# Token mix of a layer: half tiles of two batches on 64 rows each, in place of 128 rows with zeroed weights

## The chip, the cores and the metric

One core of one Trainium2 chip runs the whole program. The metric is device microseconds of one execution; the median of three runs of the kernel before is 675.2 us (674.82 to 675.28).

## What is computed

A masked attention, a gated feed-forward layer and a token-mixing layer follow one another. The part around the change is the first half of the last one, for 4 batches of 576 tokens and 512 channels:

```python
    xt = x.transpose(0, 2, 1)
    h = np.maximum(xt @ w_tok1, 0.0) @ w_tok2     # w_tok1 576 x 256, w_tok2 256 x 576
    u = x + h.transpose(0, 2, 1)
    h2 = np.maximum(u @ w_ch1, 0.0) @ w_ch2
    return (u + h2).astype(np.float32)
```

## The kernel before

**Tiles.** A float32 product is made of three matmuls on a high and a low part of each factor (mm3, line 453: high by high, high by low, low by high). The parts come from split (line 469): a copy to the high part on ScalarE (ACT) or VectorE (DVE), then a subtraction on DVE for the low part. The tokens of all batches lie in 18 tiles of 128 rows in x2. A batch has 576 tokens, four whole tiles and a half one; tile 8 holds the last 64 tokens of batch 0 in its rows 0 to 63 and those of batch 1 in its rows 64 to 127, tile 17 the same of batches 2 and 3.

**First product.** tokens_in(b) (line 892) sums w_tok1 by the tokens of a batch into two banks (hp, 128 x 512 each, m = 0 and 1) over five tiles: 6 matmuls a tile, 30 a batch. For the fifth tile there are two copies of the last 64 rows of w_tok1, each with 128 rows: t1[4] has the weights in rows 0 to 63 and zeroes below, t1[5] the other way round (lines 847 to 850; single, line 500, loads the rows and lets GpSimd (POOL) set the others to zero). So the whole half tile is multiplied, 128 rows, and what belongs to the other batch falls away. The relu of a bank is one instruction on ACT for the high part and one on DVE for the low part. In the trace the fifth tile's matmuls read wr (the split tile) with at (t1[4], batches 0 and 2) or with z (t1[5], batches 1 and 3).

**Around it.** turn(t) (line 914) transposes a token tile with four 128 x 128 transposes (cst,x or cst,y in the trace) and copies them to u. tokens_out(b) (line 929) is the second product, eight products of six matmuls with 288 columns (at,z in the trace), each added to u by DVE. The program writes them as: turns 0 to 3, tokens_in(0), turn 8, turns 4 to 7, tokens_in(1), tokens_out(0), turns 9 to 12, tokens_in(2), turn 17, tokens_out(1), turns 13 to 16, tokens_in(3), tokens_out(2), tokens_out(3).

**Order.** That is not the order of issue. All instructions go to a planner (class Plan). It knows what each depends on, and a planned cost for each (_cost, line 248). In order (line 294) every instruction of TensorE (PE) is first given the sum of the planned PE costs ahead of it in the program as its due time; then, from the back, every instruction is due no later than each of its readers less its own cost, a delay between the two engines and a pad. An engine that is free takes, of the instructions that are ready, the one with the earliest due time:

```python
            if e == "tensor":
                due[i], t = t, t + cost[i]
        for i in reversed(range(n)):
            pad = 0 if first[i] == "tensor" else 1.0
            for s in after[i]:
                due[i] = min(due[i], due[s] - cost[i] - self.TAIL[first[i]] - self.DELAY[first[i]][first[s]] - pad)
```

Only matmuls that are given to burst (line 237) stay together whatever their due times; the attention does so with its matmuls of 96 rows by 64 columns (weigh, line 620), which write the two column halves in turn. The chip's engines run their queues in the order that the planner has written.

Of the kernel before, what the change touches and what calls it, by code (L numbers as in the profile page):

```python
# [10 lines left out]
F32R = mybir.dt.float32r  # L11
# [3 lines left out]
AF = mybir.ActivationFunctionType  # L15
ALU = mybir.AluOpType
PSUM = bass.MemoryType.PSUM

B, H, S, D = 4, 8, 576, 64
C = H * D  # L20
NT = B * S
FF, HID, FF2 = 1024, 256, 1536
# [127 lines left out]
class Plan:  # L150
# [96 lines left out]
    @staticmethod  # L247
    def _cost(engine, method, kw):

        out = kw["out"]  # L250
        cols = int(np.prod(out.shape[1:]))
        pointers = sum(hasattr(kw.get(k), "space") for k in ("scale", "bias", "scalar", "scalar1"))
        if engine == "sync":
            if kw["in_"].dtype == U32:
                return max(0.45, 4 * cols * out.shape[0] / 230e3 - 0.9)
            return max(0.45, 8 * (0.03 + 4 * cols * 0.0266e-3))
        if engine == "tensor":
            if method == "transpose":
                return cols / 1200 + 0.0025
            if kw["lhsT"].dtype in (F32R, BF16):  # L260
                return cols / 2263 + 0.0049
            if kw["lhsT"].shape[0] <= D or out.shape[0] <= D:
                return cols / 1200 + 0.0025
            return 2 * max(cols / 1200 + 0.0025, 0.112)
        source = kw.get("in_", kw.get("in0"))
        psum = source is not None and "PSUM" in str(source.space)
        if engine == "scalar":
            read = 0.093 * (kw.get("accum_out") is not None)
            return (0.07 if psum else 0.1) + cols / 1200 + 0.03 * pointers + read
        if engine == "gpsimd":  # L270
            return 0.04 if method == "memset" else 0.04 + cols / 345
        if method == "tensor_reduce":
            return 0.066 + int(np.prod(source.shape[1:])) / 960
        if method == "reciprocal":
            return 0.066 + cols / 157
        fast = method in ("tensor_copy", "tensor_scalar", "tensor_scalar_add") and not psum
        return 0.066 + 0.05 * pointers + cols / (1920 if fast else 960)
# [147 lines left out]
def tile_model(nc, banks, kept_1, kept_w, kept_u, kept_mid, units, cst, mu, w_k, w_v, w_r, w_t1, w_t2, w_c1, w_c2, outT):  # L425
    memory = {k: [Slot(f"{k}{i}", n) for i, n in enumerate(v)] for k, v in SLOTS.items()}

    def f(view):
        return view.bitcast(F32)

    def at(place, shape, dtype=F32):
        name, number, offset = place
        return memory[name][number].view(offset, shape, dtype)
# [6 lines left out]
    def cut(name, numbers, size, count=None):  # L440

        out = []
        for n in numbers:
            out += [(name, n, size * i) for i in range(SLOTS[name][n] // size)]
        return out[:count]
# [7 lines left out]
    def mm3(out, lh, ll, rh, rl, first, last, goes_on=False):  # L453

        more = dict(skip_group_check=True) if goes_on else {}
        nc.tensor.matmul(out=out, lhsT=lh, rhs=rh, start=first, stop=False, **more)
        nc.tensor.matmul(out=out, lhsT=lh, rhs=rl, start=False, stop=False, **more)
        nc.tensor.matmul(out=out, lhsT=ll, rhs=rh, start=False, stop=last, **more)
# [10 lines left out]
    def split(raw, hi, lo):  # L469
        copy(hi, raw)  # L470
        combine(lo, raw, f(hi), ALU.subtract)

    def rows(n):
        return slice(128 * n, 128 * n + 128)
# [6 lines left out]
    def pair(place, shape):  # L481

        name, number, offset = place
        n = int(np.prod(shape))
        return at(place, shape, F32R), at((name, number, offset + n), shape, F32R)
# [3 lines left out]
    wr = [pair(("wr", k, 0), (C,)) for k in range(4)]  # L489
# [7 lines left out]

        return words(w).rearrange("(k p) c -> p k c", p=128)[:, :, 2 * n * m:2 * n * m + 2 * n]

    def single(srcs, t, raw_ring, zero=None):  # L500

        n = t.shape[1]
        flat = raw_ring.tile(2 * n, dtype=U32)
        for part, src in srcs:
            dst = flat[part]
            if len(src.shape) == 3:
                dst = dst.split(src.shape[1], src.shape[2])
            nc.sync.dma_start(out=dst, in_=src)
            if raw_ring is raw_a:
                nc.early[len(nc.ops) - 1] = 6  # L510
        if zero is not None:
            nc.gpsimd.memset(out=f(flat[zero]), constant=0.0)
        raw = flat.split(n, 2)
        low, h = raw[:, :, 0], raw[:, :, 1]
        b, half = t.bitcast(U32), t.bitcast(U16)
        v = nc.vector
        nc.scalar.activation(out=t, in_=f(h), func=AF.Prelu, scale=2.0 ** -112, alpha=-(2.0 ** 32))
        v.tensor_scalar(out=b, in0=b, scalar1=3, scalar2=None, op0=ALU.logical_shift_left)
        v.scalar_tensor_tensor(
            out=half, in0=low, scalar=2.0 ** -29, in1=half, op0=ALU.mult, op1=ALU.add  # L520
        )

    def weight(srcs, hi, lo, raw_ring, tmp_ring, zero=None):

        shape = tuple(hi.shape[1:])
        t = tmp_ring.tile(int(np.prod(shape)))
        single(srcs, t, raw_ring, zero)
        split(t.split(*shape) if len(shape) == 2 else t, hi, lo)

    everything = slice(0, 128)  # L530
# [121 lines left out]
    z512 = cut("z", range(5), 512)  # L652
# [4 lines left out]
    x2 = [at(place, (C,)) for place in x2_at]  # L657
# [180 lines left out]

    t1 = [pair(p, (HID,)) for p in cut("at", (1, 2), 512) + [("at", 0, 4 * S), ("at", 0, 4 * S + 512), z512[8]]]
    t2 = [pair(p, (S,)) for p in cut("at", (0,), 2 * S, 2)]
    xt512 = cut("xt", (2, 0, 1), 512)
    raw_b, tmp_b = ring(xt512[8:10]), ring(xt512[10:12])
# [1 line left out]
        weight([(everything, words(w_t1)[rows(k), :])], *t1[k], raw_b, tmp_b)  # L846
    tail = words(w_t1)[512:576, :]
    halves = [slice(0, 64), slice(64, 128)]
    for odd in range(2):
        weight([(halves[odd], tail)], *t1[4 + odd], raw_b, tmp_b, zero=halves[1 - odd])  # L850
    for k in range(2):
        for n in range(3):
            cs = slice(192 * n, 192 * n + 192)
# [8 lines left out]

    def u(b, kt, cs):
        return whole[kt // 2][:, kt % 2, S * b:S * b + S][:, cs]

    def tiles_of(b):
        base, odd = 9 * (b // 2), b % 2
        return [(base + 4 * odd + i, i) for i in range(4)] + [(base + 8, 4 + odd)]

    spots = cut("wk", range(4), 512) + cut("xt", (2, 0), 512) + cut("wr", (2,), 512) + cut("x2", (5, 6, 0, 1, 2, 3), 512)  # L870
    w1 = []
# [13 lines left out]

    for j in range(3):
        fetch_1(j)
    hid, ends = {}, {}
    hp_r, x2p_r, up_r = psum(0, 1, 2, 3), psum(4, 5), psum(6, 7)
    late_r = psum(6, 7, 4, 5)  # L890

    def tokens_in(b):
        hp = [hp_r.tile(C) for _ in range(2)]
        for n, (t, kt) in enumerate(tiles_of(b)):
            if n < 4:
                h, l = x2h_r.tile(C, dtype=F32R), x2l_r.tile(C, dtype=F32R)
            elif b % 2 == 0:
                h, l = ends[b // 2] = at(("wr", 3, 0), (C,), F32R), at(("wr", 3, 512), (C,), F32R)
            else:
                h, l = ends[b // 2]  # L900
            if n < 4 or b % 2 == 0:
                split(x2[t], h, l)
            for m in range(2):
                mm3(hp[m], t1[kt][0][:, rows(m)], t1[kt][1][:, rows(m)], h, l, n == 0, n == 4)
        hid[b] = []
        for m in range(2):
            h, l = (hid_r.tile(C, dtype=F32R) for _ in range(2))
            nc.scalar.activation(out=h, in_=hp[m], func=AF.Relu)
            nc.vector.scalar_tensor_tensor(
                out=l, in0=hp[m], scalar=0.0, in1=f(h), op0=ALU.max, op1=ALU.subtract  # L910
            )
            hid[b].append((h, l))

    def turn(t):
        tp = x2p_r.tile(4, 128)
        for kt in range(4):
            nc.tensor.transpose(out=tp[:, kt, :], in_=x2[t][:, rows(kt)], identity=ident)
        g, i = divmod(t, 9)
        for q in range(2):
            kt = slice(2 * q, 2 * q + 2)  # L920
            if i < 8:
                o = S * (2 * g + i // 4) + 128 * (i % 4)
                copy(whole[q][:, :, o:o + 128], tp[:, kt, :])
            else:
                for odd in range(2):
                    o = S * (2 * g + odd) + 512
                    copy(whole[q][:, :, o:o + 64], tp[:, kt, 64 * odd:64 * odd + 64])

    def tokens_out(b):
        for kt in range(4):  # L930
            for n in range(2):
                cs = slice(HALF * n, HALF * n + HALF)
                hp = (up_r if b < 2 else late_r).tile(HALF)
                for k in range(2):
                    h, l = hid[b][k]
                    mm3(hp, h[:, rows(kt)], l[:, rows(kt)], t2[k][0][:, cs], t2[k][1][:, cs], k == 0, k == 1)
                nc.vector.tensor_tensor(out=u(b, kt, cs), in0=hp, in1=u(b, kt, cs), op=ALU.add)
# [5 lines left out]
    for t in range(4, 8):  # L943
        turn(t)
    tokens_in(1)
    tokens_out(0)
    for t in range(9, 13):
        turn(t)
    tokens_in(2)
    turn(17)  # L950
    tokens_out(1)
    for t in range(13, 17):
        turn(t)
    tokens_in(3)
    tokens_out(2)
    tokens_out(3)

# [270 lines left out]
```

## Time and profile before

| | |
|---|---|
| median of 3 runs | 675.2 us (674.82 to 675.28) |
| the profiled execution | 676.94 us, span 675.2 us |
| TensorE (PE) matmuls busy | 659.4 us, 98% of the span |
| DVE, ACT busy | 547.1 us (81%), 332.8 us (49%) |
| token mix, from the trace | about 342 to 408 us of the span |

Times in the trace are microseconds from the start of the span. Matmuls are pipelined: a row's own duration contains the way through the array, and what one costs in a sequence is the step from start to start.

### The profile page before, as it was taken

The page shows a single profiled execution, that of the slowest core. Times are in us where ns is not written, and L with a number is a line of the kernel's source. Part 1 is how long each engine was busy: PE and PEld are TensorE (multiplying, and loading weights), DVE is VectorE, ACT ScalarE, POOL GpSimd, SP SyncE. Part 2 cuts the span into 40 slices and gives each one's busy share as a digit, 9 for nine tenths or more (in the row PEclk, how much of TensorE's full clock was granted, in tenths as well). Part 3 has the DMA queues.
Part 4 walks back from the last instruction along what each step waited for, and adds up shares of the span by engine and source line. Part 5 has one row for each costly group of instructions (what it writes and reads, how often), then busy time and mean ns, then how long its engine had stood idle before and what let it go on. Part 6 is the DMA issues. An engine that isn't in the chain of part 4 may idle for free.

```text
span 675.2 us, 11417 instructions
## 1 busy us (share of the span) xinstructions
PE 659.4 (98%) x4153; PEld 609.8 (90%) x4153; DVE 547.1 (81%) x1127; ACT 332.8 (49%) x886; POOL 2.1 (0%) x22
## 2 busy tenths in 40 slices
PE   6899999999999999999999999999998999999997
PEld 6677888888898888888878999999998999999997
DVE  4899998799689799598877659788695769998982
ACT  4989874578476467375542236563171122212310
POOL 0000000000000000000000000000000000000000
PEclk9999999999999999999999999999999999999999
DMA  8988343556656234428871356947788899632211
GB/s 315 380 318 328 108 145 108 182 160 202 189 169 193 86 138 164 160 79 313 303 252 63 95 205 240 332 174 271 249 298 334 261 390 402 219 94 93 71 36 60
DMA packets 61064, 138.06 MB, mean 204 GB/s; under 512 B 5328, under 2 KB 24656, under 8 KB 59984
## 3 DMA queue, kind: packets, MB, share of 16 engines
q1 hardware_dynamic: 61008, 137.33, 59.4%
q8 instruction: 33, 0.54, 0.3%
q14 instruction: 23, 0.19, 0.1%
HBM read 91.70 MB, written 45.61 MB: 203 GB/s over the span
## 4 chain that ended last, share of the span: by engine, by line
PE 86%; DMA 7%; DVE 3%; ACT 2%; issue 1%; SPq 0%; DVEq 0%; ACTq 0%
PE bank L411 86%; DMA x<-w_k 2%; DMA part_mid<-at 1%; DMA wr<-units 1%; ACT z L411 1%; DVE z L411 1%; DMA wv<-units 1%; DMA raw<-w_v 1%; ACT x L411 1%; DMA xt<-w_t 1%; DVE at L411 1%; DVE xt L411 0%; ACT at L411 0%; SPq L411 0%; DVE x L411 0%
## 5 line engine op out<-in xcount | busy, mean ns | idle before, releaser
L411 PE MATMUL bank<-z,wk 128*128 128x384 f32 x800 | 180.0, 343 | 1.9 <-DVE at L411 1.7
L411 PEld LDWEIGHTS bank<-z,wk 128*128 128x128 f32 x800 | 141.0, 188 | 9.3 <-DVE at L411 2.0
L411 PE MATMUL bank<-wv,z 128*128 128x512 f32 x432 | 129.4, 403 | 0.4 <-ACT z L411 0.4
L411 PEld LDWEIGHTS bank<-wv,z 128*128 128x128 f32 x432 | 78.0, 188 | 12.7 <-ACT z L411 0.8
L411 ACT ACTIVATE at<-at 128x96 f32<-128x96 f32 (+2 forms) x177 | 64.3, 365 | 24.3 <-DVE at L411 22.9
L411 PE MATMUL bank<-wr,z 128*128 128x512 f32 x228 | 62.8, 402 | 1.2 <-DVE z L411 1.2
L411 ACT ACTIVATE z<-bank 128x384 f32<-128x384 f32 (+2 forms) x60 | 29.7, 498 | 52.9 <-PE bank L411 52.6
L411 DVE TENSOR_TENSOR z<-z,z 128x384 fp32r<-128x384 f32 (+1 forms) x94 | 53.0, 569 | 3.1 <-ACT z L411 2.0
L411 PE MATMUL bank<-xt,wk 128*128 128x384 f32 x254 | 53.9, 345 | 1.3 <-ACT at L411 1.3
L411 PEld LDWEIGHTS bank<-wr,z 128*128 128x128 f32 x228 | 41.4, 188 | 8.8 <-DVE z L411 1.6
L411 DVE SCALAR_TENSOR_TENSOR z<-bank,z 128x384 f32<-128x384 f32 (+1 forms) x56 | 31.9, 573 | 21.1 <-ACT z L411 21.1
L411 PE MATMUL bank<-xt,x 128*128 128x384 f32 x248 | 48.8, 334 | 0.0
L411 PE MATMUL bank<-z,x 128*128 128x384 f32 x232 | 47.0, 334 | 0.0
L411 PEld LDWEIGHTS bank<-xt,wk 128*128 128x128 f32 x254 | 44.5, 188 | 2.5 <-issue 1.5
L411 DVE TENSOR_TENSOR at<-bank,at 128x384 f32<-128x384 f32 x64 | 35.3, 552 | 10.7 <-PE bank L411 10.4
L411 PEld LDWEIGHTS bank<-xt,x 128*128 128x128 f32 x248 | 43.5, 188 | 0.0
L411 ACT ACTIVATE z<-z 128x384 fp32r<-128x384 f32 x69 | 35.4, 523 | 11.3 <-DVE z L411 10.0
L411 PEld LDWEIGHTS bank<-z,x 128*128 128x128 f32 x232 | 40.8, 188 | 0.0
L411 ACT ACTIVATE at<-bank 128x384 f32<-128x384 f32 x35 | 17.1, 489 | 38.5 <-PE bank L411 37.6
L411 ACT ACTIVATE x<-bank 96x512 f32<-96x512 f32 (+1 forms) x48 | 28.1, 589 | 14.6 <-PE bank L411 14.3
L411 DVE SCALAR_TENSOR_TENSOR z<-xt,cst,z 128x256 f32<-128x256 f32 (+3 forms) x92 | 34.1, 404 | 0.8 <-ACT z L411 0.4
L411 ACT ACTIVATE z<-xt,cst 128x256 f32<-128x256 f32 (+3 forms) x65 | 26.6, 443 | 10.3 <-DVE z L411 9.9
(170 smaller groups left out, 1164.1 us busy)
## 6 DMA issues: line engine op xcount, KB each, us to landing
part_mid<-at SPq DMA_DIRECT2D x18, 768.0 KB, 5.0
z<-part_mid SPq DMA_DIRECT2D x11, 576.0 KB, 8.0
x<-w_c SPq DMA_DIRECT2D x12, 512.0 KB, 4.0
at<-units SPq DMA_DIRECT2D x14, 416.0 KB, 4.1
unit<-units SPq DMA_DIRECT2D x13, 416.0 KB, 4.4
at<-units SPq DMA_DIRECT2D x21, 256.0 KB, 4.1
part_w<-wv SPq DMA_DIRECT2D x21, 256.0 KB, 3.2
part_w<-x SPq DMA_DIRECT2D x21, 256.0 KB, 3.0
```

Of the source, the lines that this page charges most:

```text
L411: call(kw["out"], kw["constant"]) if method == "memset" else call(**kw)
```

## The change

The half tile is taken out of tokens_in and gets a function of its own, tokens_end(g), for the two batches of a pair. One weight, t1[4], holds the last 64 rows of w_tok1 twice, in rows 0 to 63 and 64 to 127; t1[5] and the zeroes go. The matmuls read 64 rows of weight and tile, rows 0 to 63 for the even batch and 64 to 127 for the odd one, and are written in turn for the two batches, 12 a pair. The relu of both batches stands behind them. tokens_out(0) is written after turns 9 to 12. The planned cost of a matmul with at most 64 rows is halved.

```diff
             if kw["lhsT"].dtype in (F32R, BF16):
-                return cols / 2263 + 0.0049
+                return (cols / 2263 + 0.0049) * (0.5 if kw["lhsT"].shape[0] <= D else 1)
...
-        if zero is not None:
-            nc.gpsimd.memset(out=f(flat[zero]), constant=0.0)
...
-    for odd in range(2):
-        weight([(halves[odd], tail)], *t1[4 + odd], raw_b, tmp_b, zero=halves[1 - odd])
+    weight([(half, tail) for half in halves], *t1[4], raw_b, tmp_b)
...
     def tokens_in(b):
-        hp = [hp_r.tile(C) for _ in range(2)]
...
+        hp = sums_of[b] = [hp_r.tile(C) for _ in range(2)]
+        for kt in range(4):
+            h, l = x2h_r.tile(C, dtype=F32R), x2l_r.tile(C, dtype=F32R)
+            split(x2[9 * (b // 2) + 4 * (b % 2) + kt], h, l)
             for m in range(2):
-                mm3(hp[m], t1[kt][0][:, rows(m)], t1[kt][1][:, rows(m)], h, l, n == 0, n == 4)
+                mm3(hp[m], t1[kt][0][:, rows(m)], t1[kt][1][:, rows(m)], h, l, kt == 0, False)
+
+    def tokens_end(g):
+        h, l = at(("wr", 3, 0), (C,), F32R), at(("wr", 3, 512), (C,), F32R)
+        split(x2[9 * g + 8], h, l)
+        both = list(zip((2 * g, 2 * g + 1), halves))
         for m in range(2):
+            high, low = (w[:, rows(m)] for w in t1[4])
+            for left, right, last in (high, h, False), (high, l, False), (low, h, True):
+                for b, half in both:
+                    nc.tensor.matmul(out=sums_of[b][m], lhsT=left[half], rhs=right[half], start=False, stop=last)
+        for b, _ in both:
+            hid[b] = []
+            for m in range(2):
+                h, l = (hid_r.tile(C, dtype=F32R) for _ in range(2))
+                nc.scalar.activation(out=h, in_=sums_of[b][m], func=AF.Relu)
...
     tokens_in(1)
-    tokens_out(0)
+    tokens_end(0)
     for t in range(9, 13):
         turn(t)
+    tokens_out(0)
     tokens_in(2)
...
     tokens_in(3)
+    tokens_end(1)
     tokens_out(2)
     tokens_out(3)
```

## Rows read from the trace of the kernel before

**Rows 1.** The page: busy us, share, instructions; PE and its clock by slices.
```profile
PE 659.4 (98%) x4153; PEld 609.8 (90%) x4153; DVE 547.1 (81%) x1127; ACT 332.8 (49%) x886; POOL 2.1 (0%) x22
...
PEclk9999999999999999999999999999999999999999
```

**Rows 2.** Windows: us, then PE, PEld, DVE, ACT, POOL busy; clock, DMA share, GB/s.
```profile
342.00:396.00 54.00, 53.84 (x316) 47.08 (x317) 36.31 (x78) 16.27 (x44) 0.00 (x0) 1.00 0.41 137
```

**Rows 3.** Chain of waits, in order of time: start, us, what.
```profile
342.13 9.59 PE bank L411 x49
...
351.75 140.08 PE bank L411 x836
...
500.07 9.56 DMA part_mid<-at
...
511.23 160.45 PE bank L411 x924
```

**Rows 4.** Groups of matmuls on PE: count, busy us, mean ns of one, idle before.
```profile
L411 PE MATMUL bank<-x,at 96*64 96x64 f32 x336 | 13.0, 226 | 0.0
...
L411 PE MATMUL bank<-wr,z 128*128 128x512 f32 x12 | 3.6, 391 | 0.0
L411 PE MATMUL bank<-wr,at 128*128 128x512 f32 x12 | 3.5, 412 | 0.0
```

**Rows 5.** Timeline of PE in the token mix: start, us, instruction, count.
```profile
353.99 1.17 PE L411 MATMUL bank<-wr,at 128*128 128x512 f32 x4
355.00 0.27 PE L411 MATMUL bank<-cst,x 128*128 128x128 f32 x1
355.02 0.48 PE L411 MATMUL bank<-wr,at 128*128 128x512 f32 x1
...
355.47 0.48 PE L411 MATMUL bank<-wr,at 128*128 128x512 f32 x1
...
365.66 1.07 PE L411 MATMUL bank<-wr,z 128*128 128x512 f32 x4
366.57 0.42 PE L411 MATMUL bank<-at,z 128*128 128x288 f32 x2
366.83 0.40 PE L411 MATMUL bank<-wr,z 128*128 128x512 f32 x1
...
381.09 1.52 PE L411 MATMUL bank<-wr,at 128*128 128x512 f32 x6
382.45 1.75 PE L411 MATMUL bank<-at,z 128*128 128x288 f32 x12
384.04 0.60 PE L411 MATMUL bank<-cst,x 128*128 128x128 f32 x4
384.48 0.38 PE L411 MATMUL bank<-cst,y 128*128 128x128 f32 x2
...
394.29 0.39 PE L411 MATMUL bank<-wr,z 128*128 128x512 f32 x1
...
394.75 1.30 PE L411 MATMUL bank<-wr,z 128*128 128x512 f32 x5
```

**Rows 6.** Timeline of PE around one burst of the attention.
```profile
153.54 0.58 PE L411 MATMUL bank<-at 128*128 128x96 f32 x4
154.05 1.15 PE L411 MATMUL bank<-x,at 96*64 96x64 f32 x32
155.14 1.43 PE L411 MATMUL bank<-wv,z 128*128 128x512 f32 x5
```

**Rows 7.** Timeline of ACT and PE ahead of the token mix; in brackets idle before.
```profile
341.29 0.38 ACT L411 ACTIVATE xt<-xt 128x192 f32<-128x192 f32 x1 [0.45 <-DMA xt<-w_t]
...
342.13 1.20 PE L411 MATMUL bank<-wv,z 128*128 128x512 f32 x4 [0.37 <-ACT z L411]
```

**Rows 8.** Timeline of ACT and DVE: the relu of batch 3.
```profile
395.63 1.09 ACT L411 ACTIVATE z<-bank 128x512 fp32r<-128x512 f32 x2 [6.14 <-PE bank L411]
...
396.26 1.29 DVE L411 SCALAR_TENSOR_TENSOR z<-bank,z 128x512 fp32r<-128x512 f32 x2 [1.77 <-ACT z L411]
```

More of the change, by code (lines that the diff above doesn't have):

```diff
@@ L498, in col_block, with single @@
         return words(w).rearrange("(k p) c -> p k c", p=128)[:, :, 2 * n * m:2 * n * m + 2 * n]
-    def single(srcs, t, raw_ring, zero=None):
+    def single(srcs, t, raw_ring):
         n = t.shape[1]
@@ L521, in single, with weight @@
         )
-    def weight(srcs, hi, lo, raw_ring, tmp_ring, zero=None):
+    def weight(srcs, hi, lo, raw_ring, tmp_ring):
         shape = tuple(hi.shape[1:])
         t = tmp_ring.tile(int(np.prod(shape)))
-        single(srcs, t, raw_ring, zero)
+        single(srcs, t, raw_ring)
         split(t.split(*shape) if len(shape) == 2 else t, hi, lo)
@@ L836, in tile_model @@
             attend(h, s_ring, t_ring, x_ring)
-    t1 = [pair(p, (HID,)) for p in cut("at", (1, 2), 512) + [("at", 0, 4 * S), ("at", 0, 4 * S + 512), z512[8]]]
+    t1 = [pair(p, (HID,)) for p in cut("at", (1, 2), 512) + [("at", 0, 4 * S), ("at", 0, 4 * S + 512)]]
     t2 = [pair(p, (S,)) for p in cut("at", (0,), 2 * S, 2)]
@@ L864, in u @@
         return whole[kt // 2][:, kt % 2, S * b:S * b + S][:, cs]
-    def tiles_of(b):
-        base, odd = 9 * (b // 2), b % 2
-        return [(base + 4 * odd + i, i) for i in range(4)] + [(base + 8, 4 + odd)]
     spots = cut("wk", range(4), 512) + cut("xt", (2, 0), 512) + cut("wr", (2,), 512) + cut("x2", (5, 6, 0, 1, 2, 3), 512)
@@ L887, in tile_model @@
         fetch_1(j)
-    hid, ends = {}, {}
+    hid, sums_of = {}, {}
     hp_r, x2p_r, up_r = psum(0, 1, 2, 3), psum(4, 5), psum(6, 7)
@@ L892, in tokens_in @@
     def tokens_in(b):
-        hp = [hp_r.tile(C) for _ in range(2)]
[L894 to L902, printed above, removed]
-            for m in range(2):
-                mm3(hp[m], t1[kt][0][:, rows(m)], t1[kt][1][:, rows(m)], h, l, n == 0, n == 4)
-        hid[b] = []
-        for m in range(2):
[L907 to L912, printed above, removed]
+        hp = sums_of[b] = [hp_r.tile(C) for _ in range(2)]
+        for kt in range(4):
+            h, l = x2h_r.tile(C, dtype=F32R), x2l_r.tile(C, dtype=F32R)
+            split(x2[9 * (b // 2) + 4 * (b % 2) + kt], h, l)
+            for m in range(2):
+                mm3(hp[m], t1[kt][0][:, rows(m)], t1[kt][1][:, rows(m)], h, l, kt == 0, False)
[3 more added lines that the diff above has]
+        both = list(zip((2 * g, 2 * g + 1), halves))
+        for m in range(2):
+            high, low = (w[:, rows(m)] for w in t1[4])
[7 more added lines that the diff above has]
+                nc.scalar.activation(out=h, in_=sums_of[b][m], func=AF.Relu)
+                nc.vector.scalar_tensor_tensor(
+                    out=l, in0=sums_of[b][m], scalar=0.0, in1=f(h), op0=ALU.max, op1=ALU.subtract
+                )
+                hid[b].append((h, l))
     def turn(t):
```

## Prediction

> **What bounds the kernel now.** I read the page first: in its busy table and its slices the reader is to see that TensorE (PE) is busy 98% of the span and that the granted clock never falls [rows 1]. The windows then show the token mix: from 342 to 396 us PE is idle for 0.16 us in all, while VectorE (DVE) and ScalarE (ACT) have 18 and 38 us to spare [rows 2]. The chain of waits says the same: it runs over PE alone from 342.13 to 491.83 us, leaves it for DVE, ACT and one store of 9.56 us, and returns to PE at 511.23 [rows 3]. So in this stage a microsecond of PE is a microsecond of the kernel, and what is taken from ACT, DVE or GpSimd (POOL) is worth nothing by itself.
>
> The matmuls that the change rewrites are told by their tiles: 12 read wr and at (batches 0 and 2), 12 read wr and z (1 and 3) [rows 4]. Six in a row start at 381.09 and hand over at 382.45 [rows 5], so one takes a step of 0.227 us, however long its own row says; all 24 take **5.45 us**.
>
> **The order.** What decides is the order in which the planner lets PE issue the new matmuls. It takes, of the instructions that are ready, the one with the earliest due time (lines 302 to 313 and 351 to 372). A matmul's due time is the sum of planned costs ahead of it in the program, but never later than its reader's due time less cost, delay and, for an ACT or DVE instruction, a pad of 1.0. These numbers set the order and no time. The trace shows what this does: the six of batch 0 are cut into 4, 1 and 1 by transposes that stand behind them in the program, those of batch 1 after the fourth by matmuls of tokens_out(0), those of batch 3 into 1 and 5; only batch 2's are in one piece [rows 5].
>
> Now tokens_end(1). Let E be its planned end. tokens_out(2) follows at once: its third matmul, due at E + 0.26, reads the low part of batch 2's first sum, so that low part is due at E + 0.26 - 0.60 - 0.08 - 0.20 - 1.0 = E - 1.62, the high part that it needs at E - 1.62 - 0.50 - 0.10 - 0.10 - 1.0 = E - 3.32, and the last 64-row matmul of that sum at E - 3.32 - 0.12 - 0.20 = E - 3.64. Batch 3's are read by tokens_out(3), 6.3 later, and keep their places in the program, E - 1.27 to E - 0.12. Everything of batch 2 is long ready by then. So its six matmuls aren't issued in turn with batch 3's: they go ahead on their own, among the full matmuls of tokens_in(3), which are due every 0.23 up to E - 1.62. In tokens_end(0) the same sum starts from E + 2.01 (16 transposes stand between) and gives E - 1.89 for batch 0 against E - 1.27 for batch 1. There the two banks of tokens_out(0) pull further, and matmuls of tokens_out(0) fall between those of batch 1, as they do now. **No two halves stand side by side**, so nothing overlaps.
>
> Counting by due times: batch 0's six make 3 runs of 64-row matmuls between full ones, batch 2's 4, batch 1's 4, batch 3's, with nothing due between them, 1. That is 12 runs; I would believe 9 to 15.
>
> **The sum, part by part.**
> Streaming: 24 matmuls of 512 columns, none overlapped, still 24 x 0.227 = 5.45 us: 0.
>
> Going into and out of a half array: no row shows row halves. The nearest is a burst of attention matmuls of 96 rows and 64 columns on two column halves [rows 6]. The four full ones before it, at 0.11 us each (four transposes from 384.04 to 384.48 [rows 5]), are through at 153.54 + 0.44 = 153.98. The five after it end at 155.14 + 1.43 = 156.57; one lasts 0.39 where its step is 0.227 [rows 4], so their stream ends at 156.41 and, five steps earlier, began at 155.27. Between lie 1.29 us for 16 pairs. At half of 0.11 for 64 columns a pair is 0.055, all pairs 0.88, and 0.41 remains for in and out; at the burst's own pace, less the 0.22 that one lasts [rows 4], (1.15 - 0.22) / 15 = 0.062, 0.30 remains. I take **0.35** a run. The lower end is 0, if a row half isn't such a switch: 64 of the rows is then only a smaller matmul. I take the burst's price, since it is the only work in the trace that addresses the array in parts. 12 x 0.35 = **+4.2 us** (9 x 0.30 = 2.7 to 15 x 0.41 = 6.2; at a price of 0: none). The rule that bears on it is in the Trainium skill, TensorEngine Tiling (Array Packing), section Key Properties: a change of tiling mode drains the engine, a change of tile within a mode doesn't. By it every run pays and the sum stays; no row here shows it for row halves.
>
> The weight that goes is two instructions on ACT, three on DVE and two memsets on POOL: its cover is PE, busy all through, and it comes to nothing. Both loads of the 64 rows stay on SP's queue; one tile now waits for both. One effect may reach PE: at 341.29 ACT takes up a w_t load that it had waited 0.45 us for, the split behind it came late, and PE was idle for 0.37 us [rows 7]. With one weight fewer in a ring of two buffers that load comes earlier. 0 to -0.37; neither end is nearer, so -0.2.
>
> The relu parts (ACT 0.55, DVE 0.65 us each [rows 8]): batch 0's and 2's start early, since their matmuls go ahead, so tokens_out finds them ready; batch 1's and 3's have as long as now. tokens_out(0) goes behind four turns; neither issues a DMA, so SP's queue isn't touched, and both stay among other PE work. 0; without that cover one wait of at most 0.55 + 0.65 = 1.2.
>
> Behind the mix: PE feeds the part that leaves it (the 9.56 us store and PE's idle 1.73 us at 511.23 [rows 3]), so a delay passes through; what lands beside that store may move by up to 1.7 either way. 0.
>
> Sum: +4.2 - 0.2 = **+4.0 us**. The profiled execution took 676.94 with a span of 675.2, so it would take 680.9; against the median of 675.2 I forecast **679.2**.
>
> **Rivals.**
> A, the switch costs nothing: the order is as above, but 64 rows run as a plain smaller matmul, 24 x 0.227 as before. For it: matmuls of 128 x 96, too, leave part of the array unused, and the transposes in rows 5 slip in between full ones without PE going idle. Against it: those use all rows from the first partition, while the halves are addressed as halves, and rows 6 shows a price where that is so. 675.2 - 0.2 = 675.0, no change; with 1.7 either way behind it 673.5 to 676.7.
> B, the other side: the pairs do run in turn, so the change does what it says. At the burst's 0.062 to 0.055 a pair costs 1.13 of one matmul, 0.257 us; 12 of them 3.08 in place of 5.45, two runs of 0.35, -0.2: -1.9, **673.3**. It decides as soon as a batch's six aren't pulled ahead of its partner's; the due times speak against it, and so does rows 5. In the Trainium skill, TensorE: Matmul & The Clock Gate, section Measured speedup vs the span model, four row tiles gave 3.07 times one, which is 1.30 of a matmul; as an estimate for a pair, 12 x 1.30 x 0.227 = 3.54, B would come out at 673.8.
> C, the price is between: a half needs only the way in or the way out, 12 x 0.12 to 0.18 = 1.4 to 2.2 us: 676.4 to 677.2, slower.
>
> **How the numbers follow.** About 0.2% (1.35 us) is what a measurement here can tell from no change. Forecast 0.58 (678 to 680.6), A 0.24, C 0.10, B 0.08. The likeliest gives 679.2; its own range is 678.0 to 680.6. The range for 8 in 10 takes in C and the middle of A: 674.6 to 680.6. Faster: B and a tenth of A, 0.10. Same: most of A, 0.21. Slower: the forecast, C and what of A lies above 676.55, 0.69.
>
> **What would show it.** PE's timeline of the changed kernel should have 64-row matmuls reading wr singly or by twos to sixes between 128-row ones, with neighbours of the same half, and gaps of a few tenths at each run; the stretch that was 342 to 396 should be some 4 us longer to the same work. A is right if the order is so and the steps stay at 0.227. The forecast is wrong in its first step if 64-row matmuls start in pairs a few ns apart.

## The result, and the profile after

The changed kernel took 678.61 us (median of 8 runs, 677.79 to 682.48), the kernel before on the same chip 675.24 us (8 runs): ratio **1.0056, 95% interval 1.0042 to 1.0070**. It is slower by 3.4 us. The profiled execution took 679.03 us with a span of 676.2.

The page of the changed kernel, the lines of [rows 1]:

```profile
PE 663.4 (98%) x4153; PEld 609.2 (90%) x4153; DVE 545.5 (81%) x1122; ACT 334.8 (50%) x886; POOL 1.1 (0%) x20
...
PEclk9999999999999999999999999999999999999999
```

PE has as many instructions as before and is busy 4.0 us longer. DVE has five instructions less, POOL two, and ACT as many (the prediction had put two of the five on ACT). The window of [rows 2] and the chain of waits of [rows 3] show that PE is still what everything waits for: PE has no idle time from 342 to 396 us, and one piece of the chain now holds everything from 302.08 to 672.76 us.

```profile
342.00:396.00 54.00, 54.00 (x306) 43.89 (x305) 33.90 (x71) 16.67 (x42) 0.00 (x0) 1.00 0.37 120
```

```profile
302.08 370.68 PE bank L411 x2102
```

The 64-row matmuls in the timeline of PE, against [rows 5]. The first row and the last are the ends of the token mix, turn 0's first transpose and the last product of tokens_out:

```profile
344.67 0.38 PE L411 MATMUL bank<-cst,x 128*128 128x128 f32 x2
...
356.21 1.43 PE L411 MATMUL bank<-wr,at 64*128 64x512 f32 x5
357.57 0.51 PE L411 MATMUL bank<-z,at 128*128 128x512 f32 x1
358.00 0.50 PE L411 MATMUL bank<-wr,at 64*128 64x512 f32 x1
358.43 0.74 PE L411 MATMUL bank<-z,at 128*128 128x512 f32 x2
...
365.49 0.96 PE L411 MATMUL bank<-wr,at 64*128 64x512 f32 x3
366.38 0.44 PE L411 MATMUL bank<-cst,x 128*128 128x128 f32 x2
366.74 0.50 PE L411 MATMUL bank<-wr,at 64*128 64x512 f32 x1
367.17 0.44 PE L411 MATMUL bank<-cst,x 128*128 128x128 f32 x2
367.54 0.73 PE L411 MATMUL bank<-wr,at 64*128 64x512 f32 x2
...
386.38 0.96 PE L411 MATMUL bank<-wr,at 64*128 64x512 f32 x3
387.27 0.73 PE L411 MATMUL bank<-z,at 128*128 128x512 f32 x2
387.93 0.73 PE L411 MATMUL bank<-wr,at 64*128 64x512 f32 x2
...
390.13 0.50 PE L411 MATMUL bank<-wr,at 64*128 64x512 f32 x1
...
396.76 0.73 PE L411 MATMUL bank<-wr,at 64*128 64x512 f32 x2
397.41 0.50 PE L411 MATMUL bank<-z,at 128*128 128x512 f32 x1
397.84 1.19 PE L411 MATMUL bank<-wr,at 64*128 64x512 f32 x4
398.96 8.22 PE L411 MATMUL bank<-at,z 128*128 128x288 f32 x60
...
411.07 1.05 PE L411 MATMUL bank<-at,z 128*128 128x288 f32 x6
```

Three things are to be seen. Batch 0's six come as 5 and 1, batch 1's as 3, 1 and 2, batch 2's as 3, 2 and 1, batch 3's as 2 and 4: **10 runs**, and within none of them does the other half take part. Five in a row start at 356.21 and hand over at 357.57, 1.36 us where five whole matmuls take 5 x 0.227 = 1.13. And where a single one stands between whole ones, each start is 0.43 behind the last (357.57, 358.00, 358.43), not 0.227: such a change between whole and half costs 0.2 us, going in and coming out alike. From the single instructions, 0.10 of it falls on the change and 0.11 on the step after it.

The weight loads (PEld) show what is lost there:

```profile
355.31 0.53 PEld L411 LDWEIGHTS bank<-z,at 128*128 128x128 f32 x3
356.21 0.99 PEld L411 LDWEIGHTS bank<-wr,at 64*128 64x128 f32 x5 [0.36 <-issue]
357.57 0.19 PEld L411 LDWEIGHTS bank<-z,at 128*128 128x128 f32 x1 [0.37 <-issue]
358.00 0.18 PEld L411 LDWEIGHTS bank<-wr,at 64*128 64x128 f32 x1 [0.25 <-issue]
```

Behind a change the load of the weight starts only with its own matmul (356.21, 357.57, 358.00), after PEld has been idle for 0.25 to 0.37 us. Between whole matmuls it starts a step ahead of it, as the rows of e3_full below show. How the 0.2 us divides between the load and the matmul no run separates.

Ahead of the mix ACT waited 0.64 us for the first of a pair of w_t loads (the 0.45 in [rows 7] is the wait for the second), and PE not at all:

```profile
339.98 0.38 ACT L411 ACTIVATE xt<-xt 128x192 f32<-128x192 f32 x1 [0.64 <-DMA xt<-w_t]
```

### The profile page after: what moved, and what is told of

The parts are those of the page before. It is cut to its first block, busy times and chain, and to the rows that moved or that the text cites. A ratio compares the mean times of both kernels' runs of the same rounds, so it can differ in the third digit from the quotient of the medians.

```text
span 676.2 us, 11406 instructions
## 1 busy us (share of the span) xinstructions
PE 663.4 (98%) x4153; PEld 609.2 (90%) x4153; DVE 545.5 (81%) x1122; ACT 334.8 (50%) x886; POOL 1.1 (0%) x20
## 4 chain that ended last, share of the span: by engine, by line
PE 90%; DMA 5%; ACT 2%; DVE 2%; SPq 0%; issue 0%; DVEq 0%
PE bank L411 90%; DMA x<-w_k 1%; DMA raw<-w_k 1%; DMA wr<-units 1%; DMA at<-units 1%; DMA wv<-units 1%; ACT z L411 1%; ACT x L411 1%; DVE z L411 0%; ACT at L411 0%; DVE at L411 0%; SPq L411 0%; DVE wk L411 0%; DVE x L411 0%; DVE wr L411 0%
## 5 line engine op out<-in xcount | busy, mean ns | idle before, releaser
L411 PE MATMUL bank<-wr,z 128*128 128x512 f32 x216 | 59.3, 403 | 0.9 <-DVE z L411 0.8
L411 PEld LDWEIGHTS bank<-wr,z 128*128 128x128 f32 x216 | 39.2, 188 | 8.3 <-DVE z L411 1.5
```

The costliest lines, as they stand in the source:

```text
L411: call(kw["out"], kw["constant"]) if method == "memset" else call(**kw)
```

## The experiments

All were read by the same three stretches of PE's timeline: up to turn 0's first transpose, from there to the last start of a matmul of tokens_out (the mix), and from there to the last start of any matmul (the rest). "Landing" is the time from issue to landing of the second pair of w_t loads ahead of the mix, the mean of the two, "idle" PE's wait for ACT that follows from it. All in us, the medians with the runs of the kernel before on the same chip.

| kernel | 64-row runs | landing | idle | mix from | mix | rest | median | before | ratio |
|---|---|---|---|---|---|---|---|---|---|
| before, as shown | none | 4.6 | 0.37 | 345.22 | 63.55 | 262.56 | | | |
| e0_before | none | 4.7 | 1.06 | 345.76 | 63.60 | 260.57 | 675.55 | 675.17 | 1.0002 |
| after | 10 | 4.1 | 0 | 344.67 | 67.16 | 260.57 | 678.61 | 675.24 | 1.0056 |
| e1_pairs | 2 of 12 | 6.1 | 1.77 | 346.48 | 61.63 | 260.92 | 672.85 | 675.17 | 0.9969 |
| e2_halves | 4 of 6 | 7.4 | 3.41 | 349.83 | 64.82 | 260.54 | 680.82 | 675.17 | 1.0084 |
| e3_full | none | 4.2 | 0 | 343.82 | 63.22 | 261.06 | 674.09 | 675.17 | 0.9988 |
| e4_pairs_late | 2 of 12 | 3.3 | 0 | 344.19 | 62.20 | 260.83 | 673.60 | 675.81 | 0.9967 |
| e5_before_late | none | 2.4 | 0 | 343.84 | 63.74 | 260.57 | 674.12 | 675.81 | 0.9975 |
| e6_cost | 12 | 7.1 | 2.24 | 348.61 | 68.04 | 260.55 | 683.42 | 675.81 | 1.0099 |
| e7_cost_late | 12 | 2.6 | 0 | 344.75 | 68.55 | 260.55 | 680.58 | 676.01 | 1.0069 |
| e8_halves_late | 4 of 6 | 2.4 | 0 | 343.53 | 65.46 | 260.54 | 677.22 | 676.01 | 1.0021 |

**e0_before**: the kernel before once more, for its profile.

> The kernel before once more, for a second profile of it. Every theory: 675.2 us. What it tells: whether the 1.73 us for which PE waited at 511 us, and the 0.37 us at 342 us, stand in every execution of it or came with the one that was profiled. If they belong to the kernel, the span is again near 675.2 with both waits; if not, the span is nearer to 673.5.

675.55 us, interval of the ratio 0.9989 to 1.0016. The wait of 1.73 us with which PE came back at 511.23 us, behind the store of [rows 3], isn't there, and the rest is 2.0 shorter: that wait came with one execution. PE's wait ahead of the mix is 1.06 us here where it was 0.37 [rows 7]; it differs between two executions of one kernel. In what follows e0_before is the profile to compare with.

**e1_pairs**: the twelve matmuls of tokens_end are bound together in the order of the program.

```diff
+        first = len(nc.ops)
         for m in range(2):
...
+        nc.burst(first)
```

> The changed kernel with its twelve 64-row matmuls of a pair of batches kept together as a burst, so that the halves are issued in turn. Theory 1 (neighbouring halves overlap, and each run of 64-row matmuls costs about 0.35 us to enter and leave): 12 pairs of 0.257 in place of 24 x 0.227 is -2.4, two runs +0.7, a wait for the relu of batch 2 up to 0.3: 673.5 us (672.8 to 674.4), with starts of a pair a few ns apart. Theory 2 (halves never overlap): 675.2 + 0.7 = 675.9 us, 24 starts 0.227 apart. Theory 3 (the loss comes from the order of the rest, not from the 64 rows): about 678.

672.85 us, ratio 0.9969 (0.9956 to 0.9982), in the range of theory 1. The timeline of PE, its ends and the two bursts:

```profile
346.48 0.38 PE L411 MATMUL bank<-cst,x 128*128 128x128 f32 x2
...
362.09 1.66 PE L411 MATMUL bank<-wr,at 64*128 64x512 f32 x12
...
390.96 1.65 PE L411 MATMUL bank<-wr,at 64*128 64x512 f32 x12
...
407.35 1.05 PE L411 MATMUL bank<-at,z 128*128 128x288 f32 x6
```

Twelve take 1.65 us. The tile's own view, in a window of 0.15 us, counts two starts:

```profile
L411 PE MATMUL bank<-wr,at x2: 496/496/496, 362.1 to 362.1; 64*128 64x512 f32 x2
```

The single instructions of a pair start 3 or 4 ns apart, and the next pair 0.228 to 0.236 later (0.337 for the second): a pair takes the time of one matmul. So the halves do run side by side once they are neighbours, and the order is what kept them from it.

**e2_halves**: the same binding, but batch by batch: six of one half, then six of the other.

```diff
-        for m in range(2):
...
-                for b, half in both:
+        for b, half in both:
+            first = len(nc.ops)
+            for m in range(2):
...
+            nc.burst(first)
```

> The changed kernel with the six 64-row matmuls of each batch kept together as a burst: four runs in place of ten, and within a run always the same half. Theories 1 and 2: six runs fewer at 0.35, 678.6 - 2.1 = 676.5 us (676.0 to 677.0), starts 0.227 apart. Theory 3: about 678.

680.82 us (677.98 to 683.40), ratio 1.0084 (1.0054 to 1.0113): a miss by 4 us. The mix is as expected: 64.82, 2.34 less than after with 6 runs fewer, 0.39 a run. What came on top lies ahead of it (PE's timeline, then the windows of the granted clock):

```profile
345.16 4.84 PE L411 MATMUL bank<-wv,z 128*128 128x512 f32 x13 [3.41 <-ACT z L411]
349.83 0.38 PE L411 MATMUL bank<-cst,x 128*128 128x128 f32 x2
```

```profile
344.00:346.00 2.00, 0.84 (x3) 0.70 (x4) 1.21 (x4) 1.38 (x4) 0.00 (x0) 0.90 0.44 177
346.00:348.00 2.00, 2.00 (x7) 1.52 (x6) 1.85 (x6) 0.77 (x3) 0.00 (x0) 0.50 0.06 25
348.00:350.00 2.00, 2.00 (x10) 1.59 (x8) 1.33 (x4) 0.14 (x1) 0.00 (x0) 0.75 0.35 131
```

PE stood still for 3.41 us, since ACT waited for the first w_t load of the pair, which took 7.56 us to land. After it the granted clock was 0.50, 1.2 of 2.4 GHz, and the 13 matmuls up to the first transpose took 349.83 - 345.16 = 4.67 us, where e0_before does them in 345.76 - 342.68 = 3.08.

**e3_full**: the order of issue of after, instruction by instruction, with 128 rows in every matmul. The planned cost stays halved for the matmuls of tokens_end, told by the place of their weight, so that PE gets the same order.

```diff
-                return (cols / 2263 + 0.0049) * (0.5 if kw["lhsT"].shape[0] <= D else 1)
+                w = kw["lhsT"]
+                ends = isinstance(w, View) and w.slot.name == "at0" and w.pattern[0] % w.slot.size >= 4 * S + 512
+                return (cols / 2263 + 0.0049) * (0.5 if ends else 1)
...
-                    nc.tensor.matmul(out=sums_of[b][m], lhsT=left[half], rhs=right[half], start=False, stop=last)
+                    nc.tensor.matmul(out=sums_of[b][m], lhsT=left, rhs=right, start=False, stop=last)
```

> The changed kernel, issued in the same order, but the matmuls of tokens_end read all 128 rows of weight and tile. It changes the computation: each batch's sum takes in the other batch's 64 tokens too. Theories 1 and 2 (the loss is the price of entering and leaving the half array, ten runs): 678.6 - 10 x 0.35 = 675.1 us (674.3 to 675.6). Theory 3 (the order of the rest): still about 678.6.

674.09 us, ratio 0.9988 (0.9975 to 1.0000). The timeline of PE, its ends and the place of 356.21 to 358.43 above, then the weight loads there:

```profile
343.82 0.38 PE L413 MATMUL bank<-cst,x 128*128 128x128 f32 x2
...
355.27 1.29 PE L413 MATMUL bank<-wr,at 128*128 128x512 f32 x5
356.40 0.39 PE L413 MATMUL bank<-z,at 128*128 128x512 f32 x1
356.63 0.39 PE L413 MATMUL bank<-wr,at 128*128 128x512 f32 x1
356.85 0.62 PE L413 MATMUL bank<-z,at 128*128 128x512 f32 x2
...
406.29 1.05 PE L413 MATMUL bank<-at,z 128*128 128x288 f32 x6
```

```profile
355.04 1.10 PEld L413 LDWEIGHTS bank<-wr,at 128*128 128x128 f32 x5
356.18 0.19 PEld L413 LDWEIGHTS bank<-z,at 128*128 128x128 f32 x1
```

The single one now stands 0.23 from both its neighbours, and five take 1.13. The mix is 67.16 - 63.22 = 3.94 us shorter, 0.39 for each of the 10 runs. The order, the dropped weight and the moved relu together cost nothing (674.09 against 675.17); the 64 rows between the 128 do. By the same prices the mix of e1 would be 63.22 - 12 x 0.227 + 2 x 0.39 = 61.28; it is 61.63, and the 0.35 between them stays open.

**e4_pairs_late and e5_before_late**: the three calls of fetch_1, which load the next stage's weights (part_w), are written behind tokens_in(0) in place of ahead of the mix; in e4 with the pairs of e1, in e5 in the kernel before. They are eight loads of 256 KB to 1 MB, 5.25 MB in all, and not three of 1 MB as the text on e4 has it. In the kernel before one of 1 MB is issued at 332.47 us, ahead of the second pair of w_t loads on SP's queue (335.91 and 336.51); in e4 and e5 all eight are issued behind that pair, from 336.25 and 336.59 us on.

```diff
-    for j in range(3):
-        fetch_1(j)
...
     tokens_in(0)
+    start = len(nc.ops)
+    for j in range(3):
+        fetch_1(j)
+    nc.floor.update(dict.fromkeys(range(start, len(nc.ops)), SLACK))
```

> Edit: the pairs bound in turn as in e1_pairs, and besides, the three loads of the next stage's weights (part_w, 1 MB each), which the program issues just before the token mix, are issued behind tokens_in(0). Theory 1 (what e1_pairs still lost stood ahead of the mix: PE idle for 1.77 us, since ACT waited 2.69 us for a w_t load that landed 6.1 us after its issue, behind the part_w loads on the same queue): the w_t loads land in about 2.4 us, PE isn't idle at 342 to 346, the mix stays at 61.6 us, and the time is 672.85 less 1.0 to 1.8, 671.0 to 671.9. Rival 1 (the wait is another one's, or PE is given other work by it): the idle time or its length of the mix changes by less than 0.3, 672.5 to 673.2. Rival 2: the part_w loads are then late for the first channel product, with PE idle near 400 to 420, and the time is above 673.2.

> Edit: the kernel before with the same move of the three part_w loads alone. It says what the move is worth without the half tiles. Theory 1: the w_t loads land in about 2.4 us in place of 4 to 5.3, the wait of 0.37 to 1.06 us of PE ahead of the mix goes, the mix stays at 63.6 us: 675.2 less 0.4 to 1.1, 674.1 to 674.8. Rival 1: no change, 675.0 to 675.4. Rival 2 (loads late behind the mix): slower than 675.4.

e4: 673.60 us, ratio 0.9967 (0.9950 to 0.9983). The wait is gone, but the ratio is that of e1: theory 1 fell. Its premise was the 1.77 us of e1's profile, and that was the longest of e1's 12 runs, with a span of 673.3; the median span of the twelve is 670.7. So most of e1's runs had no such wait to lose. Rival 2 isn't seen either, since PE is busy without a gap from 400 to 420 us. The mix of e4 is 0.6 us longer than that of e1, 0.14 of it idle time of PE; the rest of that stays open. e5: 674.12 us, ratio 0.9975 (0.9960 to 0.9990). The move alone is worth 1.7 us against the kernel before on the same chip, 0.6 more than the 1.1 at the end of the forecast.

**e6_cost**: the changed kernel with the planned cost of 64 rows put back.

```diff
-                return (cols / 2263 + 0.0049) * (0.5 if kw["lhsT"].shape[0] <= D else 1)
+                return cols / 2263 + 0.0049
```

> Edit: the changed kernel with the halved planned cost of a 64-row matmul put back to the full one, nothing else. By the plan it has 12 runs of 64-row matmuls between full ones in place of 10. Theory 1 (the order comes from the due times of tokens_out, which the planned cost hardly moves, and each run costs 0.39 us): a mix of 63.2 + 12 x 0.39 = 67.9 us, 0.8 more than in the changed kernel, 678.3 to 680.2 in all. Rival (the halved cost pulled the pairs apart): the halves stand side by side, a mix of 61.6 us, 672.5 to 674. Rival 2 (the price isn't one for a run but for a 64-row matmul, 24 of them at 0.164): a mix of 67.2 as in the changed kernel, 678.6.

683.42 us, ratio 1.0099 (1.0070 to 1.0128). The plan has 12 runs, ten of one or two matmuls for batches 0 and 1 and one of six each for batches 2 and 3, again with no two halves side by side. So the halved cost isn't what pulled them apart. The mix is 68.04 us against the 67.9 of theory 1 and the 67.2 of rival 2: the price is one for a run. The total missed by 3 us, again ahead of the mix: PE waited for ACT, and ACT for the first w_t load of the pair. That load is issued at 335.91 us, as in after (335.87), but lands at 343.13, not at 339.90. The planner now puts one more store (part_S) ahead of it. That this store is what delays it isn't shown: in e1, with the order and the issue times of after, the same load landed at 341.96. The windows of the granted clock, and the second pair of w_t loads in the DMA issues (KB each, median us to landing):

```profile
342.00:344.00 2.00, 0.00 (x0) 0.00 (x0) 0.35 (x2) 0.78 (x2) 0.00 (x0) 0.95 1.04 416
344.00:346.00 2.00, 1.95 (x5) 1.56 (x6) 1.97 (x7) 0.88 (x3) 0.00 (x0) 0.50 0.32 125
346.00:348.00 2.00, 2.00 (x8) 1.58 (x7) 1.37 (x3) 0.48 (x2) 0.00 (x0) 0.69 0.36 135
```

```profile
xt<-w_t SPq DMA_DIRECT2D x2, 192.0 KB, 7.1
```

**e7_cost_late and e8_halves_late**: e6 and e2 with the move of the part_w loads, as the test of whether what was missed stands ahead of the mix.

> Edit: e6_cost with the move of the three part_w loads of e4_pairs_late. Theory (e6_cost came out 3 us above its forecast by what stands ahead of the mix, not in it: the w_t load late in SP's queue behind the part_w loads, PE idle for 2.24 us and then at a granted clock of 0.50 for some 3 us, 1.6 us more): the first transpose of the mix starts at about 344.2 as in e4_pairs_late and not at 348.61, the granted clock stays at 1.00, the mix keeps its 68.0 us for 12 runs, and the time is 683.4 - 4.4 = 679.0 (678.3 to 679.7). Rival (the 12 runs themselves cost more, in or behind the mix): above 681. Rival 2 (the longer mix hides the loads that were moved, or doesn't): 0.5 either way.

> Edit: e2_halves with the same move. Theory: the idle 3.41 us ahead of the mix and the low clock behind it go, the first transpose starts at about 344.2 and not at 349.83, the mix stays at 64.8 us for its 4 runs of six, and the time is 680.8 - 5.6 = 675.2 (674.6 to 676.0), 3.2 less than e6's plan with the same move: 8 runs fewer at 0.39 each. Rival (six of one half behind six of the other cost something by themselves): above 676.5.

The same two views of e7_cost_late:

```profile
344.00:346.00 2.00, 2.00 (x15) 1.66 (x14) 1.95 (x5) 0.15 (x1) 0.00 (x0) 1.00 0.91 328
346.00:348.00 2.00, 2.00 (x12) 1.65 (x11) 1.61 (x4) 0.62 (x2) 0.00 (x0) 1.00 1.08 432
```

```profile
xt<-w_t SPq DMA_DIRECT2D x2, 192.0 KB, 2.6
```

The load lands in 2.6 us, PE isn't idle ahead of the mix, the granted clock stays at 1.00, and the mix starts 3.9 us earlier (in e8 6.3, of which 1.0 already stood at 310 us). In the profiled executions, 679.45 and 675.15 us, both came out as forecast. The medians didn't quite: 680.58 and 677.22, 2.8 and 3.6 less than without the move, where 4.4 and 5.6 were expected. The 677.22 of e8 lies where its rival was to be, above 676.5, on a chip on which the kernel before took 0.84 us longer than beside e2. The runs of e8 go from 675.15 to 682.82; what the longer ones waited for has no trace, so the rival stays open for the medians. The mixes, less 0.24 and 0.29 of idle time of PE in them, give the price once more: 68.31 - 65.17 = 3.14 for 8 runs, 0.39. Each is 0.3 us longer than without the move, and e4's 0.4 (62.06 against 61.63); why stays open. And the rows of e8 are the counterpart of e1's:

```profile
355.73 1.65 PE L411 MATMUL bank<-wr,at 64*128 64x512 f32 x6
364.59 1.65 PE L411 MATMUL bank<-wr,at 64*128 64x512 f32 x6
```

Six of one half take what twelve of both halves in turn take.

## Why the prediction was right

**The bound** held: PE without idle time in the mix, and what was taken from ACT, DVE and POOL gave nothing.

**The order** held in kind. The due times pulled each even batch's six ahead of its partner's, and no two halves met. The count was 10 runs, not 12 (batch 0 in 2, not 3; 1 and 2 in 3, not 4; 3 in 2, not 1), inside the 9 to 15 given.

**Streaming** at no gain held: behind the first step of a run, which carries the way in, the steps are 0.23 us.

**The price of a run** was mis-sized a little: 0.39 us, not 0.35, inside the 0.30 to 0.41 that the attention's column bursts gave [rows 6]. So the main term was 10 x 0.39 = 3.9 in place of 12 x 0.35 = 4.2: a price too low and a count too high nearly cancel. That the price came so near is in part luck, since it was taken from column halves of 64 columns, and no row tied them to row halves. By the rule of the Trainium skill, TensorEngine Tiling (Array Packing), section Key Properties, a change of mode drains and a change of tile doesn't. The traces agree with both halves of it: 0.39 a run, and starts 3 or 4 ns apart when the halves alternate in e1. Whether the 0.39 is a drain no run separates.

**The dropped weight** has no shown worth. The term was -0.2, at most -0.37, because the w_t load was to come earlier. It isn't issued earlier: it stands at 336.37 us in after, 336.51 in the kernel before and 336.36 in e0_before. PE's wait, 0.37 and 1.06 us with the weight, is 0 in after and e3_full, but 1.77 in e1_pairs, which drops the weight too; it follows the landing, which differs from one execution to the next. e3_full, which drops the weight and pays no runs, is 1.1 us below the kernel before; 0.4 is the mix (63.60 - 63.22), for a reason that stays open, and of the profile's lead ahead of the mix 0.7 already stood at 310 us.

**Relu and the part behind the mix** held at 0: PE went on without a gap, and the rest is 260.57 us in after and e0_before. The ±1.7 us given for the store at 500 us belonged to one execution of the kernel before.

Sum: +4.0 forecast, +3.4 measured. The terms of profiles alone, after against e0_before: -1.1 ahead of the mix, +3.6 in it, 0.0 behind, +2.5; of the 0.9 to the medians 0.35 lies outside the span (time less span is 2.13 in the median of the changed kernel's runs and 1.78 in those of e0_before), and the rest is less than executions of one kernel differ by (spans of e0_before from 672.1 to 675.1).

**The rivals.** A, that the switch costs nothing, is refuted by e3_full: same order, 3.94 us less in the mix. C, one way only at 1.4 to 2.2 us, falls with these 3.94 us and with the rows of after, where both ways cost 0.2. B didn't happen, but e1_pairs makes it happen and shows its price: 672.85 against the 673.3 worked out, 2.3 us below the kernel before where 1.9 was worked out. The pair was priced too high, 0.257, from a burst of 64 columns; with 512 it is 0.23. The 1.30 of a matmul that the prediction worked out for a pair from the Trainium skill, TensorE: Matmul & The Clock Gate, section Measured speedup vs the span model, isn't what two halves show here: 0.231 is 1.02 of 0.227.

## What to carry to other kernels

The two row halves of the array paid here only as neighbours, so look at the order in which they are issued, not at that in which the program writes them: where a planner goes by due times, bind the pair. Price every run of partial matmuls with its way in and out, here 0.39 us, 1.7 whole matmuls of 512 columns: by these numbers a run of one pair would save 0.23 and lose 0.39, and six pairs in one run save 1.36 and lose 0.39. And before a wait of a profile is made the reason of a change, compare that execution's span with those of the other runs.

## What the runs showed that was not expected

- The way in and the way out each cost twice: 0.10 us at the change and 0.11 on the following step, and at each the weight load no longer ran ahead.
- Two halves lose nothing by each other: 12 matmuls in 1.65 us, as 6 of one half.
- A pair of loads of 192 KB took 2.4 to 3.3 us in the mean to land where the part_w loads were moved behind it, and 4.1 to 7.4 us where a part_w load of 1 MB was issued 3 to 4 us ahead of it. In e2 and e8, the far ends, 5.0 us of the start of the mix go with it: 3.41 us of idle PE and 1.6 us of lower clock.
- With PE standing still for 2.24 us (e6_cost) or 3.41 us (e2_halves) the granted clock fell to 0.50 (1.2 GHz) for some 3 us, and 13 matmuls took 1.5 to 1.6 us longer; with 1.77 us (e1_pairs) it stayed at 1.00 in the windows.
- The fastest are the pairs bound together, 0.9969 and 0.9967 of the time before, with or without the move of the loads; the two gains don't add.
